# Attention over eight rows on one core: two finished key slots take row 7's layer 1 values, and every engine's order is written anew

## The chip, the core and the metric

The kernel runs on one of the eight cores of a Trainium2 chip. The core has TensorE (PE in the profile; PEld is its weight load), VectorE (DVE), ScalarE (ACT), GpSimd (POOL) and SyncE (SP), which here only issues DMAs. They run beside each other and wait for each other through semaphores. The metric is the device time of one execution in microseconds, as the median of several runs. Before the change it is 232.87 us (three runs: 232.79, 232.87 and 234.93).

## What is computed

Eight rows (a decode step: one token each) go twice through attention over a window of 1024 cached keys and values, and twice through a small dense block. Both attention layers use the same caches and weights.

```python
# x: [8, 1, 448]; k_cache, v_cache: [8, 8 heads, 4096, 256]; wq: [448, 4096]; wo: [4096, 448]
# w1: [448, 1792]; w2: [1792, 448]; everything is bf16
def A(x, k_cache, v_cache, wq, wo):
    q = (x @ wq) as [8, 16 heads, 1, 256]
    k, v = the last 1024 positions of the caches, each head used by two of q's
    p = softmax(q k^T / 16)
    return (p v) as [8, 1, 4096] @ wo
def B(x, w1, w2):
    return silu(x @ w1) @ w2
x = x + A(layernorm(x)); x = x + B(layernorm(x))      # layer 1
x = x + A(layernorm(x)); x = x + B(layernorm(x))      # layer 2
```

## The kernel before

Row by row, 8 key loads and 8 value loads of 512 KB go into a ring of 30 slots in SBUF (`slots`, line 456 issues the loads). SP issues them in a fixed order, and a load waits until the slot that it overwrites has been read for the last time. Row b's keys serve layer 1 and layer 2 of that row before they are freed; row 6's and row 7's slots are never overwritten, as no load follows them.

The program is a list of tasks. Each names the buffers that it reads and writes, from which `Plan` derives the waits, and `Plan.schedule` puts the tasks of each engine in an order that is written out by hand in `ORDER`: one character for each task, the place of the next task in the list of those that are left (in the order in which the program adds them). An engine works strictly in this order. A task whose input is late therefore holds everything behind it on its engine.

What a row does, with the names that the orders below use (a name with `:b` belongs to row b):

- `KT0` to `KT7` (line 632, DVE): two transposes for each key slot, in place, as soon as its load has landed.
- `S0.0`, `S0.1` (648, PE): the scores of layer 1 for the heads' first and second half; `S1.0`, `S1.1` those of layer 2. Each half is four groups of matmuls.
- `max`, `mT`, `mg`, `mb` (665 to 669, DVE), `exp` (672, ACT), `perm` (674, PE), `turn` (676, DVE), `l` (680, PE), `rl` (690, DVE): the softmax, with a 0 for layer 1 and a 1 for layer 2.
- `PVA` (729, PE): the values of heads 0 to 3. `PVD` (748): heads 4 to 7, one group of four matmuls a head. For rows 6 and 7 `PVC` takes heads 4 to 6, and `PVc` (760) head 7. `PV1.0` and `PV1.1` (729) are layer 2's values of the row before.
- `oevA`, `oevC`, `oevD`, `oev1` (715 and 723, ACT): copy the values from PSUM to SBUF; `oTA`, `oTC`, `oTD`, `oT1` (702, PE) turn them by a selection matmul; `oTev` (696, DVE) scales them. A and C work in two halves, `.0` and `.1`.
- `woA`, `woD`, `woC` (801, PE) and `woc` (816): the output projection; `rowb1` (1091, ACT), `fold1` (501, PE).
- `xb1` (827, DVE), `stat1` (834, PE), `var1` (837, ACT), `pow1` (839, POOL): norm; `w1` (518, PE), `yT` (538, DVE), `tanh` (846, ACT), `hT` (847, DVE), `w2` (865, PE), `rowb2` (869, ACT), `fold2`: the dense block. Then `xb2`, `stat2`, `wq0` and `wq1` (892, PE), `qT` (538, DVE), `qm` (901, DVE), `qd` (905, PE) and `qbd2` (909, ACT) make layer 2's queries, which `S1.0` waits for.
- `zero` (853, PE): matmuls whose result nobody reads.

At the start the norm and the queries of all eight rows are made together: `xb0` (576, DVE), `sq8` (547, ACT), `sqh8` (548 and 549, DVE), `stat8` (553), `x0` (580 to 587, DVE), `q1` (591, PE), `q1r`, `q1T`, `q1s` (595, 597, 610, DVE), `qbd1` (622, POOL). Constants are filled in by `init`, `initb` (a whole PSUM bank), `initq`, `inits` and `initz` on DVE. Sums over the rows of `wo` and `w2` are made once: `rsum` (443, ACT), `rsum2` and `rsum3` (435, DVE), and `rsumd` (438 and 447) writes them into the weights; `woD:0` and `w2:0` need them.

At the end, rows 0 to 6 go through their last projection and dense block together (`wo8`, `w18`, `z8`, `h8` at line 979, `w28` at 983, `xres8` at 988, `rowb9` at 991, `fold9` at 992, `orow8` at 994), and row 7 by itself (`woL`, `foldL`, `statL`, `w1L`, `w2L`, `orowL`).

The edited function is `o_turn`. With `halves`, its two copies go to `e_sb`. For layer 1 (`g` is None and `L` is 0) that is `E_sb[0]` for both halves, a part of `qbd[0]`, which had held the exponentials of layer 1: the second copy must wait until the first selection has read it.

Of the kernel before, what the change touches and what calls it, by code (L numbers as in the profile page):

```python
# [14 lines left out]

ORDER = {
    "pe": (
        "0000001000000000101111112222000200066000028827222010111117777000002444422100017777161551002010044000"
        "1005550000111117777000030444443200011661144410011101054000006055000011111777700003044443220001110033"
        "3302201100044000177005000011111777700040044444321001111444410201110100330010605500001111177770004004"  # L20
        "4444320001115144441001110110330010660500300111177770004004444322012228882041002222200004400000666600"
        "00cccc0000000500044443220001107066605504401200f0033bbb4390200500020144033555500111222244442211412321"
        "05044000100"),
    "dve": (
        "22Ca9BknxkDvv23iy1ArgCCCSk7Awodxr706t6Dtb1EDzBrraml2twi3l6hfhgl31o3kfaec2232ba99288442f514a403943822"
        "61203010098909706065ab09a90087700555504000100088909806065ab0a990087700555550000100088980878060aba0a9"
        "0087700555550000110a08989078060aba0ab0088700555550000100098980778005ab099b00777005555500001000989807"
        "78005aa0b9b00777005555500001000a90989078060aaba099a900005555500001100aaiba0cf0c8ba070600444030200002"
        "0111333311122211110000"),
    "act": (  # L30
        "0022223313333133d33b43222224211000000000201112100000000022011100000000002201100000000000220110000000"
        "00002201100000000000220111110000000002201100100000403020001110001010"),
    "pool": (
        "00000301022000110220022002200200001000"),
}


# [164 lines left out]
def bass_interleave_layers__sliding_block_cached__dense_activation_silu__decode_kernel(  # L202
# [3 lines left out]
    _, HKV, SK, DH = A_k_cache.shape  # L206
# [18 lines left out]
    LAST = NB - 1  # L225
# [10 lines left out]
    slots = [sb(f"slot{i}", [P, 2048], BF16) for i in range(R)]  # L236
# [44 lines left out]
    def QB(i, k2):  # L281
        return [("qbd", i, k2)]

    def bk(i):
        return [("bank", i)]

    def SL(s, h=None):
        return [("slot", s, 0), ("slot", s, 1)] if h is None else [("slot", s, h)]
# [4 lines left out]
    def dve(fn, reads, writes, row, name):  # L293
        add("dve", fn, reads=reads, writes=writes, row=row, name=name)

    def act(fn, reads, writes, row, name):
        add("act", fn, reads=reads, writes=writes, row=row, name=name)
# [152 lines left out]
    slot_of = {}  # L450
# [241 lines left out]
    def o_out(b, tb, n, o_c, dst, h0, keys, name, rk):  # L692
        if dst is None:
            act(lambda e: e.activation(o2[b], bank[tb][:, o_c:o_c + 2 * n], ACTF.Copy), bk(tb), keys, b, "oTc" + name)
            return
        dve(lambda e: e.tensor_tensor(  # L696
            dst, bank[tb][:, o_c:o_c + 2 * n].rearrange("p (a n) -> p a n", a=2),
            rl[b][:, h0:h0 + n].unsqueeze(1).broadcast_to([P, 2, n]), ALU.mult),
            bk(tb) + rk, keys, b, "oTev" + name)

    def o_sel(tb, src, s, sel_o, o_c, n, reads, b, name):
        pe([lambda e, a=a, s=s: e.matmul(bank[tb][:, o_c + a * n:o_c + (a + 1) * n], src(s)[:, a:DH:2], sel_o(s),  # L702
                                         start=(s == 0 and a == 0), stop=(s == 1), skip_group_check=True)
            for s in ((0, 1) if s is None else (s,)) for a in range(2)], reads + ["ident", "selb"], bk(tb), b, name)

    def o_turn(b, L, n, sel_o, o_c, dst, h0, keys, name, halves, g=None):

        pb, tb, qi, rk = (OB[L], LB[L], L, [("rl", b)]) if g is None else \
            ((OB[1], SC[1])[g], (LB[1], OB[1])[g], g, [("rlg", g)])
        ob = bank[pb]  # L710
        if halves:
            for s in range(2):
                e_sb, k = (E_sb[qi], QB(qi, 1)) if g is None or s == 0 else (pT_sb[qi], QB(qi, 0))
                if g is None or s == 0:
                    act(lambda e, s=s, e_sb=e_sb: e.activation(e_sb, ob[:, s * DH:(s + 1) * DH], ACTF.Copy), bk(pb), k, b,  # L715
                        "oev%s.%d" % (name, s))
                else:
                    dve(lambda e, s=s, e_sb=e_sb: e.tensor_copy(e_sb, ob[:, s * DH:(s + 1) * DH]), bk(pb), k, b,
                        "oev%s.%d" % (name, s))
                o_sel(tb, lambda s, e_sb=e_sb: e_sb, s, sel_o, o_c, n, k, b, "oT%s.%d" % (name, s))  # L720
        else:
            full = qbd[L][:, 8:8 + 2 * DH]
            act(lambda e: e.activation(full, ob[:, :], ACTF.Copy), bk(pb), QB(L, 0) + QB(L, 1), b, "oev" + name)  # L723
            o_sel(tb, lambda s: full[:, s * DH:(s + 1) * DH], None, sel_o, o_c, n, QB(L, 0) + QB(L, 1), b, "oT" + name)
        o_out(b, tb, n, o_c, dst, h0, keys, name, rk)
# [8 lines left out]
    def pv_first(b):  # L734
        lists = [pv(b, 0, j, j, 0, 8, 2 + 2 * j, 2, "") for j in range(4)]
        for i in range(4):
            pe([l[i] for l in lists], [k for kvh in range(4) for k in SL(slot_of[b, "v", kvh])] + QB(0, 0), bk(OB[0]), b,
               "PVA")
        o_turn(b, 0, 8, lambda s: view(ident[:], s, [(32, 4), (2, 2)]), C_O, oT1[b][:, :, 0:8], 0,
               [("oT1", b, kvh) for kvh in range(4)], "A", True)  # L740

    def pv_late(b, k0, k1, name):

        n = k1 - k0
        for i, kvh in enumerate(range(k0, k1)):
# [415 lines left out]
```

## Time and profile before

| | us |
|---|---|
| median of three runs | 232.87 |
| the profiled execution | 234.52 |
| its span on the core | 232.6 |
| TensorE busy | 168.7 |
| VectorE busy | 157.6 |
| ScalarE busy | 66.6 |
| POOL busy | 22.9 |
| transfers: mean rate over the span | 336 GB/s |

In the profile's text a line such as L632 is a line of the kernel, `slot<-slot` are the tiles written and read, and an arrow behind a row names what ended the idle time before it. The granted clock is the share of TensorE's full clock that it was given.

### The profile page before, as it was taken

Reading aid. Unit: us, or ns where it says so; the run is one execution under the profiler, and the core shown is the slowest. Engines: PE = TensorE matmul, PEld = TensorE weight load, DVE = VectorE, ACT = ScalarE, POOL = GpSimd, SP = SyncE. Lnnn points to the kernel's source line nnn. Section 1 sums busy time; section 2 is a strip of 40 time slices with the busy share of each in tenths; the row PEclk is TensorE's granted clock in tenths of the full one; section 3 lists DMA queues with packets and bytes.
Section 4 is the critical chain, followed back from the end, with each engine's and each line's share of the span. In section 5 each row is a group of like instructions: output and inputs, shape, how many; then the busy total and the mean of one; then the engine's idle time right before and its main releaser. Section 6 shows DMA issues by size and latency. Waiting matters only on the chain.

```text
span 232.6 us, 8240 instructions
## 1 busy us (share of the span) xinstructions
PE 168.7 (73%) x3648; PEld 95.8 (41%) x3648; DVE 157.6 (68%) x422; ACT 66.6 (29%) x203; POOL 22.9 (10%) x42
## 2 busy tenths in 40 slices
PE   1000526158897987988798889778888997999994
PEld 1000513112464444445444644444355465566553
DVE  5009899993983697498568747864996598354742
ACT  2000000997213322232332133223321431243321
POOL 1000201001100200020020002000200101001200
PEclk9999999656999999999999999999999999999999
DMA  6999999999999999999999999999999999600000
GB/s 155 387 409 410 380 380 399 405 409 410 403 392 386 413 405 352 391 411 408 359 402 409 405 359 407 410 370 379 409 409 387 409 380 407 229 0 6 3 1 4
DMA packets 23401, 78.20 MB, mean 336 GB/s; under 512 B 3127, under 2 KB 6086, under 8 KB 22982
## 3 DMA queue, kind: packets, MB, share of 16 engines
q1 hardware_dynamic: 22806, 77.30, 85.7%
q8 instruction: 28, 0.46, 0.8%
q10 hardware_dynamic: 560, 0.38, 0.8%
q14 instruction: 7, 0.06, 0.1%
HBM read 77.67 MB, written 0.01 MB: 334 GB/s over the span
## 4 chain that ended last, share of the span: by engine, by line
PE 45%; DMA 19%; ACT 13%; DVE 13%; SPq 5%; issue 4%; DVEq 0%
DMA w_sb<-in_B_w_dram 12%; PE bank L648 10%; DMA slot<-in_A_k_cache_dram 7%; PE bank L729 7%; DVE slot L632 6%; PE bank L892 6%; ACT slot L443 6%; PE bank L801 4%; SPq L456 3%; PE bank L518 3%; PE bank L865 2%; PE bank L748 2%; DVE bank L538 2%; PE bank L905 2%; ACT qbd L672 2%
## 5 line engine op out<-in xcount | busy, mean ns | idle before, releaser
L632 DVE STREAM_TRANSPOSE slot<-slot 128x512 uint32<-128x512 uint32 x128 | 81.6, 682 | 13.7 <-DMA slot<-in_A_k_cache_dram 13.2
L648 PE MATMUL bank<-slot,qbd 128*16 128x256 bf16 (+1 forms) x1024 | 39.4, 286 | 7.3 <-ACT qbd L909 3.3
L648 PEld LDWEIGHTS bank<-slot,qbd 128*16 128x16 bf16 (+1 forms) x1024 | 23.4, 88 | 17.4 <-ACT qbd L909 6.7
L729 PE MATMUL bank<-slot,qbd 128*4 128x512 bf16 (+1 forms) x384 | 26.9, 389 | 2.3 <-DVE qbd L676 1.6
L839 POOL TENSOR_TENSOR fcols<-fcols 128x1 f32<-128x1 f32 x17 | 9.5, 556 | 92.0 <-ACT fcols L837 81.9
L591 PE MATMUL bank<-slot,wq_sb 128*128 128x16 bf16 x128 | 3.6, 174 | 19.9 <-DVE slot L584 19.9
L622 POOL TENSOR_TENSOR qbd<-q1s,fcols 128x256 bf16<-128x256 bf16 x16 | 9.6, 614 | 85.7 <-PE bank L702 79.4
L892 PE MATMUL bank<-wq_sb,xbz 128*2 128x256 bf16 x512 | 16.1, 275 | 0.0
L909 ACT ACTIVATE qbd<-bank 128x256 bf16<-128x256 f32 x16 | 6.1, 384 | 34.2 <-PE bank L905 34.2
L696 DVE TENSOR_TENSOR q1s<-bank,q1s 128x16 bf16<-128x16 f32 (+1 forms) x18 | 3.0, 166 | 19.0 <-PE bank L702 19.0
L853 PE MATMUL bank<-ident,cols 128*128 128x512 bf16 x48 | 15.4, 387 | 0.0
L801 PE MATMUL bank<-wo_sb,q1s 128*1 128x449 bf16 x248 | 15.3, 377 | 0.2 <-ACT wo_sb L447 0.2
L715 ACT ACTIVATE qbd<-bank 128x256 bf16<-128x256 f32 x22 | 8.4, 383 | 18.9 <-PE bank L729 14.7
L443 ACT ACTIVATE slot<-w_sb 128x448 bf16<-128x448 bf16 x6 | 3.5, 576 | 35.6 <-DMA w_sb<-in_B_w_dram 35.4
L729 PEld LDWEIGHTS bank<-slot,qbd 128*4 128x4 bf16 (+1 forms) x384 | 8.2, 85 | 13.0 <-issue 3.1
L676 DVE STREAM_TRANSPOSE qbd<-bank 128x256 bf16<-128x256 bf16 x17 | 8.1, 476 | 8.0 <-PE bank L674 7.7
L538 DVE STREAM_TRANSPOSE bank<-bank 128x256 f32<-128x256 f32 (+1 forms) x25 | 10.8, 433 | 3.0 <-PE bank L892 1.1
L892 PEld LDWEIGHTS bank<-wq_sb,xbz 128*2 128x2 bf16 x512 | 11.7, 82 | 2.0
L591 PEld LDWEIGHTS bank<-slot,wq_sb 128*128 128x128 bf16 x128 | 3.5, 104 | 20.0 <-DVE slot L584 20.0
L723 ACT ACTIVATE qbd<-bank 128x512 bf16<-128x512 f32 x13 | 7.7, 595 | 11.7 <-PE bank L748 9.4
L665 DVE TENSOR_REDUCE mm<-bank 128x1 f32<-128x256 f32 x17 | 7.1, 418 | 5.5 <-PE bank L648 5.2
L748 PE MATMUL bank<-slot,qbd 128*12 128x512 bf16 (+3 forms) x120 | 9.9, 412 | 0.0
(163 smaller groups left out, 238.3 us busy)
## 6 DMA issues: line engine op xcount, KB each, us to landing
slot<-in_A_k_cache_dram SPq DMA_DIRECT2D x64, 512.0 KB, 8.4
slot<-in_A_v_cache_dram SPq DMA_DIRECT2D x64, 512.0 KB, 10.7
wo_sb<-in_A_wo_dram SPq DMA_DIRECT2D x1, 3584.0 KB, 26.0
wq_sb<-in_A_wq_dram SPq DMA_DIRECT2D x3, 1024.0 KB, 9.3
w_sb<-in_B_w_dram SPq DMA_DIRECT2D x1, 1568.0 KB, 28.3
w_sb<-in_B_w_dram SPq DMA_DIRECT2D x1, 1344.0 KB, 17.7
wq_sb<-in_A_wq_dram SPq DMA_DIRECT2D x1, 256.0 KB, 3.6
wq_sb<-in_A_wq_dram ACTq DMA_DIRECT2D x1, 256.0 KB, 4.0
```

Source lines behind the costliest of these rows:

```text
L443: act(lambda e, i=i, a=a: e.activation(junk, w[:, i * PW + R0 + a * D:i * PW + R0 + (a + 1) * D], ACTF.Copy, scale=-1.0 / D, accum_out=sum ...
L538: dve(lambda e: e.transpose(view(bank[bi][:], n, [(2, n // 32), (n // 16, 16), (1, 2)]), bank[bi][:, 0:n].rearrange("p (g r s) -> p g r s" ...
L622: pool(lambda e, k2=k2: e.tensor_tensor(qdata(0, k2), q1s[:, b, 64 * k2:64 * k2 + 64].rearrange("p (n r) -> p n r", r=2).unsqueeze(3) .bro ...
L632: dve(lambda e, v=v: e.transpose(v, v), SL(s, h), SL(s, h), b, "KT%d" % k)
L648: fns.append(lambda e, w=w, j=j, kv=kv, cb=cb, par=par: e.matmul(sc[32 * j:32 * j + up_to, 0:256], w, kv, start=(cb == 0 and par == 0), st ...
L715: act(lambda e, s=s, e_sb=e_sb: e.activation(e_sb, ob[:, s * DH:(s + 1) * DH], ACTF.Copy), bk(pb), k, b, "oev%s.%d" % (name, s))
L729: return [lambda e, u=u: e.matmul(bank[OB[L] if ob is None else ob][32 * j:32 * j + 2 * n, :], pT_sb[L if qi is None else qi][:, pcol(u, c ...
L748: pe([lambda e, t=t, c0=c0, w=w, kvh=kvh: e.matmul(bank[OB[0]][32 * t:32 * t + 2 * w, :], pT_sb[0][:, pcol(2 * t, c0):pcol(2 * t, c0) + 2 ...
L801: fns.append(lambda e, i=i, w=w, c0=c0: e.matmul(bank[XB][32 * (i % 4):32 * (i % 4) + 1, c0:c0 + D + 1], oT(i), w, start=(i < 4), stop=(i ...
L839: pool(lambda e: e.tensor_tensor(rhalf, var4, nhalf, ALU.pow), ["var4", "nhalf"], ["rhalf"], b, "pow" + name)
L853: pe(lambda e: e.matmul(bank[SC[1]][:, :], cols[:, 3:4].broadcast_to([P, P]), view(ident[:], 0, [(0, 4), (1, P)]), start=True, stop=True), ...
L892: pe([lambda e, j=j, c=c, s=s, wb=wb, k2=k2: e.matmul(bank[wb][32 * j:32 * j + 2, 0:256], pair(b, xcol(c, k2), s), view(wq_sb[:], c * HD + ...
```

## The change

Two things change. In `o_turn`, for row 7 in layer 1, the two halves of A go to the two halves of the slot that held row 6's key 6, and those of C to the slot of key 7. Layer 2 of row 7 and all other rows keep their buffers. And the four order strings are new: 238 of 511 places on PE hold another task than before, 232 of 422 on DVE, 25 of 168 on ACT and 12 of 38 on POOL. SP's order stays.

```diff
 ORDER = {
     "pe": (
-        "0000001000000000101111112222000200066000028827222010111117777000002444422100017777161551002010044000"
-        "1005550000111117777000030444443200011661144410011101054000006055000011111777700003044443220001110033"
-        "3302201100044000177005000011111777700040044444321001111444410201110100330010605500001111177770004004"
-        "4444320001115144441001110110330010660500300111177770004004444322012228882041002222200004400000666600"
-        "00cccc0000000500044443220001107066605504401200f0033bbb4390200500020144033555500111222244442211412321"
-        "05044000100"),
+        "000u000011110000002220110011151000100033399300611110111117777000030233332210011055040333302010003302"
+        "8010550000111117777000033033332200011666611002201120044000177716000001111777700704003333220001166151"
+        "4002201101044000177716000001111777700040044442320001161551400220110100022017771600000111177770004004"
+        "4442320001166114444100110000330017771611110111177770004004444232012228882041002222200000330017777102"
+        "00cccc00000005000444423200011880066660044012000033ccc43a02060500020144033555502h01122224444221131121"
+        "61551000000"),
     "dve": (
-        "22Ca9BknxkDvv23iy1ArgCCCSk7Awodxr706t6Dtb1EDzBrraml2twi3l6hfhgl31o3kfaec2232ba99288442f514a403943822"
...
+        "1iRJLBqN.17rcA10xExZpk0CT3rTqqiQgxxxh43flGgruunBtppC6rnvpnglsbkknbqpbbdl51h0dded68l76113c66668639a33"
...
     "act": (
-        "0022223313333133d33b43222224211000000000201112100000000022011100000000002201100000000000220110000000"
-        "00002201100000000000220111110000000002201100100000403020001110001010"),
+        "0022223313333423d33b42221111311000000000220110100000000022011000000000002201100000000000220110000000"
+        "00002201100000000000220111100000000002201000100000403020001111001000"),
     "pool": (
-        "00000301022000110220022002200200001000"),
+        "00000301022002200301022003010301001000"),
 }
...
         if halves:
             for s in range(2):
                 e_sb, k = (E_sb[qi], QB(qi, 1)) if g is None or s == 0 else (pT_sb[qi], QB(qi, 0))
+                if b == LAST and L == 0:
+                    sl = slot_of[LAST - 1, "k", 6 if name == "A" else 7]
+                    e_sb, k = slots[sl][:, 1024 * s:1024 * s + DH], SL(sl, s)
                 if g is None or s == 0:
```

What the strings say, read off for the stretches that matter below (`*4` is four in a row; `-` before, `+` after; fills left out where the line says so).

DVE from the first instruction to the first maximum, without `init`, `initb`, `initq`, `inits` and `initz`:

```text
- xb0 sqh8*2 KT1 st8*3 KT0 x0 KT3*2 KT0 KT2 x0*2 KT1 KT5 x0 st8 KT2 KT7 KT5 q1r q1T x0 KT4*2 q1s KT6*2 KT7 rsum3 max0
+ KT1*2 KT0 KT2 KT3 xb0 sqh8*2 KT2 st8 x0*2 KT3 x0 st8 KT6 x0 KT4 x0 st8 KT5 st8 x0 KT0 KT7*2 KT6 KT4 q1r q1T KT5 q1s rsum3 rsum2 max0
```

Before the first `KT1` stand 24 instructions in the old order and 8 in the new; between it and `max0` stand 62 and 78. After `max0` the old order mixes `rsum2` and `rsum3` with `mT0`, `mg0` and `mb0`; the new one has the three at once, then `turn0` and two `rsum3`. On ACT the first `exp0` stands behind six `rsum` of `w2` in both.

DVE in row 2 from the first norm to the queries, and PE in row 2:

```text
- xb1 KT2*2 KT3 yT KT3 hT KT4 KT5 KT4 xb2 KT6 KT5 qT0
+ xb1 KT2*2 yT KT3 hT KT3 KT4 KT5 xb2 KT6 KT5 KT6 qT0
- oTA.1 PVD*2 PV1.0*2 PVD*2 PV1.0*2 PV1.1 oTD woA woD PV1.1*3 fold1 zero oT1 w1 stat1 zero*4 w2 S0.0 fold2 S0.0*2 stat2 wq0 wq1 qd0 S0.0 S1.0*4
+ oTA.1 PVD*2 PV1.0*4 PVD*2 woA oTD PV1.1*2 woD PV1.1*2 zero fold1 oT1 stat1 w1 zero*3 w2 S0.0*3 fold2 S0.0 zero stat2 wq0 wq1 qd0 S1.0*4
```

PE in the other rows, from the late values to the projection:

```text
row 0 - PVD*4 xinit woA oTD zero woD fold1 zero stat1 w1 zero*4 w2
      + PVD*3 zero PVD woA oTD woD zero fold1 zero*2 stat1 w1 w2
row 1 - PVD PV1.0*4 PVD PV1.1 PVD PV1.1*2 PVD woA oTD PV1.1 woD
      + PVD*2 woA PV1.0*2 PVD PV1.0 PVD PV1.0 PV1.1*3 oTD PV1.1 woD
row 3 - PVD*3 woA PVD PV1.0*4 oTD PV1.1*2 woD PV1.1*2
      + PVD*2 PV1.0*2 PVD PV1.0 PVD PV1.0 woA oTD PV1.1*2 woD PV1.1*2
row 4 - PVD*4 PV1.0*4 oTD woA PV1.1 woD PV1.1*3
      + PVD*2 PV1.0 PVD PV1.0*2 PVD PV1.0 woA oTD PV1.1*2 woD PV1.1*2
row 5 - PVD*3 PV1.0 PVD PV1.0*3 PV1.1 oTD woA woD PV1.1*3
      + PVD*2 PV1.0*2 PVD*2 PV1.0*2 PV1.1*2 oTD woA woD PV1.1*2
row 6 - fold2 stat2 wq0 wq1 S0.1:7*4
      + fold2 zero wq1 stat2 wq0 S0.1:7*4
```

Row 7: ACT's copies, PE around them, and the end on PE:

```text
- oevA.0 exp1:6 oevA.1 oevC.0 lc1:6 oevC.1      + oevA.0 exp1:6 oevA.1 lc1:6 oevC.0 oevC.1
- oTA.1 PVC*2 woA PV1.0 PVC PV1.0*3 oTC.0 PV1.1*2 oTC.1 PV1.1*2 woC PVc
+ oTA.1 PVC*2 PV1.0*2 woA PVC PV1.0*2 PV1.1*2 oTC.0 oTC.1 PV1.1*2 woC PVc
- w28 xres8 perm1a l1a ... woLa xinitL fold9 zero foldL zero*2 statL w1L xres zero w2L zero
+ w28 perm1a xinitL xres8 l1a ... woLa zero foldL zero*2 statL fold9 w1L xres w2L zero*2
```

`h8` on DVE stands before `mT1a` in the old order and behind `mg1a` in the new one.

More of the change, by code (lines that the diff above doesn't have):

```diff
@@ L23 @@
-        "05044000100"),
-    "dve": (
-        "22Ca9BknxkDvv23iy1ArgCCCSk7Awodxr706t6Dtb1EDzBrraml2twi3l6hfhgl31o3kfaec2232ba99288442f514a403943822"
[L26 to L29, printed above, removed]
+        "000u000011110000002220110011151000100033399300611110111117777000030233332210011055040333302010003302"
@@ new lines @@
+        "8010550000111117777000033033332200011666611002201120044000177716000001111777700704003333220001166151"
[3 more added lines that the diff above has]
+        "61551000000"),
+    "dve": (
+        "1iRJLBqN.17rcA10xExZpk0CT3rTqqiQgxxxh43flGgruunBtppC6rnvpnglsbkknbqpbbdl51h0dded68l76113c66668639a33"
+        "63563440c0aa2199170055aa0c9a0078700555550000110089908708065ba0a990077700555550002000088880770605ab0c"
+        "aa0077700555550000000908889077005ab09a9007770055555000000090a980877005ab09aa007870055555000000090888"
+        "9078005aa09b900987005555500000000990988078060bcaa0ab990000555550000100bdc0aafc09c09a0806004440302000"
+        "022201333312122211110000"),
```

## The prediction

> **What bounds the kernel now.** I read the page first, then the chain of waits, the waits of the engines, and last the timeline in the stretches that the chain names.
>
> ```profile
> span 232.6 us, 8240 instructions
> PEclk9999999656999999999999999999999999999999
> GB/s 155 387 409 410 380 380 399 405 409 410 403 392 386 413 405 352 391 411 408 359 402 409 405 359 407 410 370 379 409 409 387 409 380 407 229 0 6 3 1 4
> PE 45%; DMA 19%; ACT 13%; DVE 13%; SPq 5%; issue 4%; DVEq 0%
> slot<-in_A_k_cache_dram SPq DMA_DIRECT2D x64, 512.0 KB, 8.4
> DVE slot L632 <- DMA slot<-in_A_k_cache_dram: 13.2, 2, 12.1
> ```
>
> The stream of keys and values runs at some 410 GB/s until it ends in the 35th slice. At that rate a load of 512 KB takes 1.28 us and the 16 loads of a row 20.5 us. Yet the chain is 45% TensorE and only 19% transfers, and VectorE waited for a key slot only twice, 12.1 of 13.2 us being the first key of all. So a row is paced by its own chain of work, with the transfers just ahead of it. The chain in order of time shows this, and below it stands one stretch of the table of windows (TensorE, weight loads, VectorE, ScalarE and POOL busy, granted clock, transfers):
>
> ```profile
> 55.60 1.45 PE bank L801 x14
> 87.73 0.39 ACT qbd L909
> 99.34 1.30 DVE slot L632 x2
> 109.11 0.39 ACT qbd L909
> 130.25 0.39 ACT qbd L909
> 143.83 1.99 DVE slot L632 x3
> 152.07 0.39 ACT qbd L909
> 173.83 0.39 ACT qbd L909
> ```
>
> ```profile
> 40.27:55.46 15.19, 7.40 (x62) 2.26 (x62) 11.74 (x20) 14.78 (x51) 0.34 (x1) 0.59 1.02 407
> ```
>
> The first release of layer 2's queries (L909) marks each row. The distances are 21.4, 21.1, 21.8 and 21.8 us: 0.9, 0.6, 1.3 and 1.3 over the 20.5 of the stream. Before them ScalarE, which sums weight rows (L443), is busy 14.78 of the 15.19 us up to 55.46, and then releases row 0's projection (L801, 55.60).
>
> **The change part by part.** The profiled execution took 234.52 us, of which its span is 232.6; the three runs have a median of 232.87 (232.79 to 234.93). I sum differences against the span and put them on the median.
>
> *The buffer.* Row 7's four copies (two in A, two in C) go to slots of row 6's keys 6 and 7, so the second copy of a pair need not wait for the selection matmul that reads the first. No instruction is added.
>
> ```profile
> 200.63 0.38 ACT L715 ACTIVATE qbd<-bank 128x256 bf16<-128x256 f32 x1 [2.38 <-PE bank L729]
> 200.91 0.47 ACT L672 ACTIVATE qbd<-bank,mm 128x256 bf16<-128x256 f32 x1
> 201.36 0.38 ACT L715 ACTIVATE qbd<-bank 128x256 bf16<-128x256 f32 x1
> 204.56 0.38 ACT L715 ACTIVATE qbd<-bank 128x256 bf16<-128x256 f32 x1 [0.31 <-PE bank L702]
> 205.56 0.74 PE L801 MATMUL bank<-wo_sb,q1s 128*1 128x449 bf16 x12
> ```
>
> In pair A the exponential of row 6 (200.91, 0.47) stands between the copies in ScalarE's order, before and after. It ends at 201.38 and the second copy starts then anyway: nothing is gained, and if the exponential were gone the copy would wait for the first selection. In pair C the second copy waited 0.31 us for TensorE. That wait goes; the copy of row 6's sums (L687) also moves ahead of the pair. TensorE then has both selections after two value groups and one gap less: I take 0.2 us of the 0.31 off L801 at 205.56. Writing a slot is costed at zero: the copy has the same shape, and every reader of those keys stands before it in TensorE's order. A slower write would be bounded by one copy, 0.38.
>
> *The last 15 us.* Two moves cost there. The last fold of rows 0 to 6 (L992) moves from before row 7's fold to between the variance and the up projection; the activation h8 (L979) moves behind two softmax steps, so the down projection of rows 0 to 6 (L983) starts later.
>
> ```profile
> 218.88 0.94 PE L983 MATMUL bank<-w_sb,slot 128*7 128x448 bf16 x14
> 225.72 0.35 PE L992 MATMUL bank<-slot 128*7 128x448 bf16 x1
> ```
>
> L983 (218.88) moves back about 0.3, an estimate from the steps that h8 now waits for, but the permutation behind it waits for ScalarE's exponential anyway, and the residual matmuls now follow that permutation instead of preceding it: +0.05. The fold takes 0.35 of TensorE's time, partly hidden where it stands, since row 7's fold waits there for ScalarE; where it goes nothing hides it but the overlap of two matmuls: +0.1. Together with the pair, the tail comes to -0.05, between -0.3 (all of 0.31) and +0.6 (both moves in full, no gain).
>
> *The start.* Before the first key's transpose VectorE now has 8 instructions instead of 24. The norm of all rows (xb, L576, and its two squares) is put behind five transposes.
>
> ```profile
> 4.38 0.20 DVE L576 TENSOR_TENSOR xb<-bank,fcols 128x40 bf16<-128x40 f32 x1
> 5.09 0.19 DVE L549 TENSOR_TENSOR slot<-slot 128x32 bf16<-128x32 f32 x1
> 17.36 0.71 DVE L632 STREAM_TRANSPOSE slot<-slot 128x512 uint32<-128x512 uint32 x1 [12.08 <-DMA slot<-in_A_k_cache_dram]
> 18.13 0.06 DVE L331 MEMSET fcols<- 32x4 f32 x1
> 18.93 0.48 DVE L331 MEMSET bank<- 128x512 f32 x1
> 39.40 0.42 DVE L665 TENSOR_REDUCE mm<-bank 128x1 f32<-128x256 f32 x1
> 40.27 2.02 DVE L435 TENSOR_REDUCE slot<-w_sb 128x4 f32<-128x1792 bf16 x1
> 44.35 0.46 ACT L672 ACTIVATE qbd<-bank,mm 128x256 bf16<-128x256 f32 x1
> 196.04 0.41 DVE L665 TENSOR_REDUCE mm<-bank 128x1 f32<-128x256 f32 x1
> 196.94 0.21 DVE L669 STREAM_TRANSPOSE mm<-mg 128x32 f32<-128x32 f32 x1
> ```
>
> ```profile
> 17.36:39.40 22.04, 8.21 (x224) 6.48 (x224) 20.80 (x63) 0.00 (x0) 2.85 (x3) 1.00 1.04 391
> ```
>
> From 17.36 to the first maximum (39.40) VectorE ran 63 instructions, busy 20.80 of 22.04 us. In the new order 79 stand there: a weight sum that is now ahead of the maximum (2.0), the norm with its round trip to ScalarE (4.38 to 5.28: 0.9), two bank fills (0.5 each), a dozen small fills (0.06 to 0.1 each, say 0.8), less three moved behind (0.6). That is 4.1 us: the maximum comes at 43.5. The three steps after it take 1.1 us with it in row 7 (196.04 to 197.15), so the exponential can start at 44.65. ScalarE reaches it at 44.35. So a delay that looks like 4 us costs 0.3, since ScalarE had its sums to do; and all behind it on ScalarE, up to the release at 55.60, moves by the same 0.3. With the weight sums that VectorE still owes I take 0.4. The ends are 0 (the fills overlap better; a gain is excluded, since ScalarE had no idle time there to give back) and 2.5 (in the rivals). The same order puts one small weight step before row 0's first turn: +0.15. Start: +0.55.
>
> *Row 2.* Here the old order put the variance matmuls (L834) behind the up projection, and VectorE's third key behind a late transfer.
>
> ```profile
> 101.06 0.95 PE L518 MATMUL bank<-w_sb,xbz 128*2 128x224 bf16 x32
> 101.93 0.25 PE L834 MATMUL bank<-xbz 128*128 128x1 bf16 x4
> 102.53 0.39 DVE L538 STREAM_TRANSPOSE bank<-bank 128x224 f32<-128x224 f32 x1
> 103.21 0.27 ACT L846 ACTIVATE th<-bank,fcols 128x14 f32<-128x14 f32 x1 [0.72 <-POOL fcols L839]
> 103.59 0.17 DVE L847 SCALAR_TENSOR_TENSOR q1s<-th,bank 128x14 bf16<-128x14 f32 x1
> ```
>
> L518 ended at 102.0 but was turned at 102.53, and the tanh waited 0.72 us for POOL's power of that late variance. The new order has the variance first and two transposes, not three, before the turn. The turn can start at 102.2, the tanh at 102.65, and L847 follows one transpose (0.71 as at 17.36) at 103.2: -0.4. One transpose more stands before the query turn, so the gain could shrink to 0.1; I keep -0.4.
>
> *Rows 1 and 3 to 6.* Groups of value matmuls change places with the output projection.
>
> ```profile
> 118.40 1.03 PE L729 MATMUL bank<-slot,qbd 128*8 128x512 bf16 x16
> 117.42 0.93 PE L801 MATMUL bank<-wo_sb,q1s 128*1 128x449 bf16 x16
> ```
>
> Four groups take 1.03, so one takes at most 0.26 us; the projection takes 0.93 less its overlap, say 0.8. Row 1's last late-value group had seven groups of row 0 ahead of it; now three and a projection: -0.1. Row 3 is nearly level (-0.1). Row 4 had its four late groups together; now three others come among them (up to +0.6), but the same work stood behind them before the projection could start, so +0.15. Row 5 has one more ahead: +0.1. Row 6 keeps its groups; its second query half goes first while the variance waits, and VectorE's transposes end both at 194.8. I call these rows 0, between -0.6 and +0.6. No load changes its place in SP's queue: value slots come free a few groups earlier or later, under 1 us, against the 8.4 us from issue to landing that the page shows where a load alone would need 1.28, so several loads stand ahead of each.
>
> *Sum.* +0.55 - 0.4 + 0 - 0.05 = +0.1, against a span of 232.6; on the median I say 232.9 us: no change that can be told.
>
> **The rivals.**
>
> *Slower: the norm behind the keys.* The point of decision is ScalarE's 44.35. The durations of the old 63, added up row by row from 17.36 to 39.40, make 24.2 us, and they took 22.0. If the new 79 don't overlap, they take 24.2 + 4.1 = 28.3: the maximum is at 45.7, the exponential at 46.85. ScalarE stands 2.5 us, and all of row 0 moves. With +0.15 and -0.4 - 0.05 that is 232.87 + 2.2 = 235.1. Against it: the old ones did overlap.
>
> *Slower: TensorE stays cold.* In the slices from 40.7 to 58.2 the granted clock was 0.6, 0.5 and 0.6, and full after. By the row of 40.27 to 55.46 it was 0.59 while TensorE was busy 7.40 of 15.19. The new order takes one filler matmul from between row 0's last selection and its projection, and four from behind L518. If the clock rises later, L518 (0.95 in row 2) takes twice as long, with the folds around it some +1.3 us: 234.2. The Trainium skill (TensorE: Matmul & The Clock Gate, Part 1, What's actually happening) says that the clock doubles after a busy window of about 3.4 us and falls after an idle one, in windows that run freely. By that rule a hole ahead of row 0 can cost one whole window; the trace agrees so far as the clock was down from the slice at 40.7 us, and up again only when TensorE's work had closed up by 58 us.
>
> *Faster: the rows fall to the stream's pace.* If the new orders take out what the four distances have over 20.5 us (0.9 + 0.6 + 1.3 + 1.3 = 4.1), the time is 228.9. For it: 99.34 and 143.83 are transposes behind late transfers, which a shorter row would release sooner. Against it: only row 2 has a wait that the order visibly removes.
>
> *The edit does nothing.* Pair C's wait of 0.31 becomes idle time in front of L801, as pair A's already is, and the orders cancel: 232.9 to 233.2.
>
> **How the numbers follow.** Forecast 0.60 (232.9, its own range 231.9 to 234.0, from the ends of rows and tail); no effect 0.08; norm late 0.13; cold clock 0.07; stream's pace 0.12. About 1% (2.3 us) is what a measurement of this kernel can tell from no change: faster takes the stream's pace, 0.12; slower half of the norm's, which lies at the bound of 235.2, and as much for it or the other losses together with the cold clock, 0.12; the same 0.76. The range leaves out most of the fastest case and the slow end: 231.2 to 234.8.
>
> **What would show it.** In the changed profile the first exponential on ScalarE starts at 44.4 to 45.2, with an idle time before it under 1 us, and the output projection of row 0 at 55.8 to 56.4. In row 2 the tanh no longer waits for POOL. L715's fourth copy in row 7 follows the third at once, the second still follows the exponential. The row marks lie 21 to 21.8 apart. I am wrong if ScalarE idles over 2 us ahead of that exponential, if the granted clock is half beyond 58 us, or if the marks come 20.5 apart.

## The result and the profile after

| | before | after |
|---|---|---|
| median of 20 runs | 234.39 us (231.87 to 236.12) | 235.14 us (234.03 to 237.65) |
| ratio, with its 95% interval | | 1.0065 (1.0040 to 1.0089) |
| profiled execution, its span | 234.52, 232.6 | 234.37, 232.6 |

The change makes the kernel slower by 1.5 us by the ratio (0.0065 of 234.39; 0.9 to 2.1), and by 0.75 between the two medians. The ratio is taken over the executions that were not slow as a whole, and is not the quotient of these medians. The loss is small, less than the 1% that the prediction called a change that can be told, but its interval leaves out 0, and the forecast had no change. Note also that the kernel before, run 20 times, stands at 234.39 and not at the 232.87 of the three runs on which the forecast was put. The forecast of 232.9 misses 235.14 by 2.2 us, and about two thirds of that is this base.

The profiled executions are no help at their ends: both spans are 232.6, because the one of after is among its shortest. They have to be read stretch by stretch. From the page of the changed kernel:

```profile
span 232.6 us, 8240 instructions
PEclk9999999956999999999999999999999999999999
GB/s 162 391 407 411 380 381 397 408 407 409 411 362 306 411 408 392 364 414 409 391 387 413 409 348 407 409 404 405 407 410 387 405 394 404 225 3 3 3 4 1
PE 55%; DVE 20%; ACT 11%; issue 5%; DMA 5%; SPq 1%; DVEq 0%
```

Two things differ from before. The chain's share of transfers fell from 19% to 5% and VectorE's rose from 13% to 20%. And the transfers, which ran at 392 and 386 GB/s in the 12th and 13th slice, now dip to 362 and 306 there: slots of the first row come free later (SP issues the keys that follow at 70.43 us, and at 68.67 before). The chain of waits in order of time says where VectorE came in. First the start of the chain before, then of the chain after (start, length, what):

```profile
11.95 28.30 DMA w_sb<-in_B_w_dram
40.27 0.68 ACT slot L443 x2
```

```profile
4.29 12.62 DMA slot<-in_A_k_cache_dram
16.94 0.71 DVE slot L632
...
37.55 0.69 DVE q1s L610
...
42.86 1.88 DVE slot L435
...
46.95 0.68 ACT slot L443 x2
...
57.06 0.96 PE bank L804 x15
```

Before, the first 40 us hang on one thing: the load of w2, whose rows ScalarE then sums, until row 0's projection (the 55.60 of the prediction). After, the chain goes from the first key through VectorE's whole list to the first exponential, and only then joins ScalarE's sums. The timeline of the changed kernel has the join, and the windows view has VectorE's work ahead of it (TensorE, weight loads, VectorE, ScalarE and POOL busy, clock, transfers):

```profile
39.51 0.58 ACT L443 ACTIVATE slot<-w_sb 128x448 bf16<-128x448 bf16 x1 [16.16 <-DMA w_sb<-in_B_w_dram]
42.77 1.96 DVE L435 TENSOR_REDUCE slot<-w_sb 128x4 f32<-128x1792 bf16 x1
44.65 0.41 DVE L665 TENSOR_REDUCE mm<-bank 128x1 f32<-128x256 f32 x1
45.79 0.47 ACT L672 ACTIVATE qbd<-bank,mm 128x256 bf16<-128x256 f32 x1 [2.11 <-DVE mm L669]
```

```profile
16.94:44.65 27.71, 9.51 (x242) 7.27 (x242) 25.07 (x79) 4.25 (x13) 2.85 (x3) 1.00 1.04 395
```

ScalarE is done with six sums at 43.68 and stands 2.11 us for the softmax's last step on VectorE. The exponential comes at 45.79 instead of 44.35, row 0's projection at 57.06 instead of 55.60. From the one to the other it is 11.27 us, and 11.25 before: what stands behind the exponential moves with it.

The two profiles close as follows. Layer 2's queries of row 0 are released at 67.17 instead of 66.23 (+0.94; the projection itself took less time after). From there to row 6's release it is 129.13 instead of 130.24 (-1.11), row 7's part takes 19.18 instead of 19.40 (-0.22), and from there to the last output it is 14.92 instead of 14.54 (+0.38). The rows of the first and last releases, before and after:

```profile
66.23 0.38 ACT L909 ACTIVATE qbd<-bank 128x256 bf16<-128x256 f32 x1 [2.24 <-PE bank L905]
...
196.47 0.38 ACT L909 ACTIVATE qbd<-bank 128x256 bf16<-128x256 f32 x1 [3.13 <-PE bank L905]
...
215.87 0.39 ACT L909 ACTIVATE qbd<-bank 128x256 bf16<-128x256 f32 x1 [1.76 <-PE bank L905]
```

```profile
67.17 0.38 ACT L912 ACTIVATE qbd<-bank 128x256 bf16<-128x256 f32 x1 [2.07 <-PE bank L908]
...
196.30 0.38 ACT L912 ACTIVATE qbd<-bank 128x256 bf16<-128x256 f32 x1 [2.69 <-PE bank L908]
...
215.48 0.38 ACT L912 ACTIVATE qbd<-bank 128x256 bf16<-128x256 f32 x1 [1.69 <-PE bank L908]
```

The middle is not what it seems, though: most of the 1.11 is two rows of the old kernel that stalled in this one execution (below).

### The profile page after: what moved, and what is told of

Same layout as the page of the kernel before. It is cut to its first block, busy times and chain, and to the rows that moved or that the text cites. A ratio compares the mean times of both kernels' runs of the same rounds, so it can differ in the third digit from the quotient of the medians.

```text
span 232.6 us, 8240 instructions
## 1 busy us (share of the span) xinstructions
PE 169.5 (73%) x3648; PEld 95.0 (41%) x3648; DVE 158.1 (68%) x422; ACT 66.1 (28%) x203; POOL 22.9 (10%) x42
## 4 chain that ended last, share of the span: by engine, by line
PE 55%; DVE 20%; ACT 11%; issue 5%; DMA 5%; SPq 1%; DVEq 0%
PE bank L648 11%; DVE slot L632 9%; PE bank L732 9%; PE bank L895 6%; PE bank L804 5%; DMA slot<-in_A_k_cache_dram 5%; PE bank L751 4%; ACT qbd L672 3%; PE bank L856 3%; PE bank L518 3%; ACT slot L443 2%; PE bank L674 2%; ACT rowb L1094 2%; PE bank L702 2%; PE bank L908 2%
## 5 line engine op out<-in xcount | busy, mean ns | idle before, releaser
L732 PE MATMUL bank<-slot,qbd 128*4 128x512 bf16 (+1 forms) x384 | 27.6, 388 | 1.0 <-DVE qbd L676 0.8
L895 PE MATMUL bank<-wq_sb,xbz 128*2 128x256 bf16 x512 | 16.6, 275 | 0.2 <-DVE xbz L830 0.2
L856 PE MATMUL bank<-ident,cols 128*128 128x512 bf16 x48 | 16.3, 392 | 0.0
L912 ACT ACTIVATE qbd<-bank 128x256 bf16<-128x256 f32 x16 | 6.1, 383 | 33.8 <-PE bank L908 33.8
L538 DVE STREAM_TRANSPOSE bank<-bank 128x256 f32<-128x256 f32 (+1 forms) x25 | 11.0, 440 | 2.6 <-PE bank L518 2.1
L718 ACT ACTIVATE qbd<-bank 128x256 bf16<-128x256 f32 x18 | 6.9, 381 | 15.9 <-PE bank L732 14.5
L751 PE MATMUL bank<-slot,qbd 128*12 128x512 bf16 (+3 forms) x120 | 10.5, 411 | 0.0
L868 PE MATMUL bank<-w_sb,q1s 128*1 128x449 bf16 x98 | 6.5, 353 | 4.9 <-DVE q1s L850 4.9
L672 ACT ACTIVATE qbd<-bank,mm 128x256 bf16<-128x256 f32 x17 | 8.0, 470 | 6.7 <-DVE mm L669 6.1
```

Source lines behind the costliest of these rows:

```text
L538: dve(lambda e: e.transpose(view(bank[bi][:], n, [(2, n // 32), (n // 16, 16), (1, 2)]), bank[bi][:, 0:n].rearrange("p (g r s) -> p g r s" ...
L672: act(lambda e: e.activation(E, x, ACTF.Exp, bias=m[:, 0:1], scale=1.0, **acc), bk(si) + [("mm", si)], QB(qi, 1) + ([] if acc == {} else [ ...
L732: return [lambda e, u=u: e.matmul(bank[OB[L] if ob is None else ob][32 * j:32 * j + 2 * n, :], pT_sb[L if qi is None else qi][:, pcol(u, c ...
L751: pe([lambda e, t=t, c0=c0, w=w, kvh=kvh: e.matmul(bank[OB[0]][32 * t:32 * t + 2 * w, :], pT_sb[0][:, pcol(2 * t, c0):pcol(2 * t, c0) + 2 ...
L856: pe(lambda e: e.matmul(bank[SC[1]][:, :], cols[:, 3:4].broadcast_to([P, P]), view(ident[:], 0, [(0, 4), (1, P)]), start=True, stop=True), ...
L895: pe([lambda e, j=j, c=c, s=s, wb=wb, k2=k2: e.matmul(bank[wb][32 * j:32 * j + 2, 0:256], pair(b, xcol(c, k2), s), view(wq_sb[:], c * HD + ...
```

## The experiments

**Which part of the change.** The new orders split cleanly where the same tasks are done in both: the start (up to row 0's second fold), the end (from row 7's first projection), and the rows between.

```diff
 new start:  - old, old, old      + start new, rows old, end old
 new end:    - old, old, old      + start old, rows old, end new
 new rows:   - old, old, old      + start old, rows new, end old  (old buffers)
 old start:  - new, new, new      + start old, rows new, end new  (new buffers)
```

> The kernel before with the new order of the start alone (VectorE up to row 1's first keys, TensorE up to row 0's second fold, ScalarE up to row 0's last weight sum). Theory 1 (the loss is the start: VectorE reaches the first maximum late and ScalarE stands about 2 us ahead of the first exponential): +0.9 to +1.6 us on the kernel before, and row 0's projection at about 57 us. Theory 2 (the loss is the new orders of rows 1 to 6): +-0.3. Theory 3 (the loss is the end, where the activation of rows 0 to 6 and the last fold have moved): +-0.3, and the late start is eaten by the transfers that run ahead.

> The kernel before with the new order of the end alone (TensorE from row 7's first projection, VectorE and ScalarE from row 7's dense block). Theory 1: 0 to +0.4 us. Theory 2: +-0.2. Theory 3: +1.0 to +1.6.

> The kernel before with the new orders between these two alone (rows 1 to 6 and row 7's layer 1; the old buffers). Theory 1: -0.8 to 0 us, as row 2's and row 4's waits go. Theory 2: +0.9 to +1.6. Theory 3: +-0.4.

> The changed kernel (new buffers too) with the old order of the start. Theory 1: -0.6 to +0.2 us against the kernel before, so 1 us or more under the changed kernel. Theories 2 and 3: +1.0 to +1.6, as the changed kernel.

Against the kernel before (233.86 us in these runs): new start 1.0087 (1.0048 to 1.0125), which is +2.0 us; new end 1.0014 (0.9973 to 1.0055); new rows 1.0003 (0.9963 to 1.0042); the changed kernel with the old start 0.9974 (0.9935 to 1.0013), which is -0.6. Put alone, the start brings the whole loss, and taken out of the change, the loss is gone. Theories 2 and 3 fall. The size was missed: +2.0 lies above the +0.9 to +1.6 of theory 1, and the +0.1 of the new rows just above its -0.8 to 0. The new start alone has the idle time of the changed kernel, and a little more:

```profile
39.59 0.58 ACT L443 ACTIVATE slot<-w_sb 128x448 bf16<-128x448 bf16 x1 [15.78 <-DMA w_sb<-in_B_w_dram]
...
46.26 0.47 ACT L672 ACTIVATE qbd<-bank,mm 128x256 bf16<-128x256 f32 x1 [2.50 <-DVE mm L669]
```

**What in the start.** Four kernels change VectorE's list only, against the kernel before or the new start.

```diff
 new VectorE start (TensorE and ScalarE old)
-  VectorE: old list
+  VectorE: new list
 sum ahead (from the kernel before)
-  rsum3 max0 mT0 rsum2 mg0 mb0 rsum3 rl0 turn0
+  rsum3 rsum3 max0 mT0 rsum2 mg0 mb0 rl0 turn0
 sum behind (from the new start)
-  rsum3 ... rsum2 max0 mT0 mg0 mb0 rsumd turn0 rsum3
+  rsum3 ... max0 mT0 mg0 mb0 rsum2 turn0 rsumd rsum3
 norm first (from the new start)
-  8 fills, KT1, 8 fills, KT1 KT0 KT2 KT3 ... xb0 sqh8*2 ...
+  7 fills, 9 fills that the norm needs, xb0 sqh8*2, KT1, ...
```

> The kernel before with the new start, but VectorE's one weight sum of w2 that the new order has ahead of the first maximum stands behind the softmax's last step (as does its write into the weights). The norm and the queries stay as late as in the new start. Theory 1a (what costs is only how much work VectorE has in its order ahead of the first exponential): first maximum at about 42.7 us, ScalarE idle under 0.4 us ahead of the exponential, 0 to +0.5 us on the kernel before. Theory 1b (the late norm and queries cost by themselves, through TensorE's late scores): +1.2 to +2.0, as the new start. Theory 1c (the new start's orders of TensorE and ScalarE cost): +1.2 to +2.0.

> The kernel before, in which one weight sum of VectorE (2.9 us) is moved from behind the first softmax to ahead of its maximum; norm, queries, fills and all other engines stay. Theory 1a: the last softmax step ends at about 45.5 instead of 42.6, ScalarE reaches the exponential at 44.35 and stands some 1.1 us, and the time is +0.9 to +1.5 us. Theories 1b and 1c: +-0.3.

> The kernel before with the new start, but the norm (three instructions) and the nine fills that it needs stand ahead of the first key's transpose, in time that VectorE idles anyway. This takes about 2.7 us of work out of the stretch ahead of the maximum; the weight sum stays ahead of it. Theory 1a: maximum at about 42, ScalarE idle under 0.4 us, 0 to +0.4 us on the kernel before. Theory 1b: the same. Theory 1c: +1.2 to +2.0.

> The kernel before with VectorE's new start alone (one small fill of the denominators' columns stands a little earlier, as TensorE's old order needs it); TensorE and ScalarE keep the old order. Theories 1a and 1b: +1.2 to +2.0 us. Theory 1c: -0.3 to +0.4.

| kernel | ratio (95% interval) | us | ScalarE idle ahead of the exponential | exponential after ScalarE's first sum |
|---|---|---|---|---|
| before | 1 | 0 | 0 | 4.08 |
| new start | 1.0087 (1.0048 to 1.0125) | +2.0 | 2.50 | 6.67 |
| new VectorE start | 1.0085 (1.0047 to 1.0123) | +2.0 | 2.36 | 6.54 |
| changed kernel | 1.0065 (1.0040 to 1.0089) | +1.5 | 2.11 | 6.28 |
| sum ahead | 1.0033 (0.9994 to 1.0073) | +0.8 | 1.52 | 5.69 |
| sum behind | 1.0045 (1.0012 to 1.0079) | +1.1 | 0.93 | 5.11 |
| norm first | 1.0013 (0.9992 to 1.0033) | +0.3 | 0 | 4.15 |

The last column is the fair one, as w2 lands at another time in each execution (39.2 to 40.6 over the profiles). The new VectorE list alone costs as much as the whole new start, so the orders of TensorE and ScalarE are out (theory 1c). The time goes up with how late the exponential is, whichever instruction is put ahead of it. The rate is only roughly known, 0.5 to 1.0 us per us: 2.0 for 2.59 in the new start, 0.8 for 1.61 in sum ahead, 1.1 for 1.03 in sum behind. In sum ahead nothing but one weight sum has moved; the norm and the queries are where they were. Its +0.8 is a little under the +0.9 to +1.5 of theory 1a and has an interval that just reaches 0, so by itself it would not settle it:

```profile
39.17 0.58 ACT L443 ACTIVATE slot<-w_sb 128x448 bf16<-128x448 bf16 x1 [34.34 <-DMA w_sb<-in_B_w_dram]
...
44.86 0.47 ACT L672 ACTIVATE qbd<-bank,mm 128x256 bf16<-128x256 f32 x1 [1.52 <-DVE mm L669]
```

Sum behind gave back about half. Theory 1a expected nearly all (0 to +0.5 us, ScalarE idle under 0.4) and theory 1b nothing, so neither is right alone. Its timeline says why:

```profile
38.20 0.69 DVE L610 CAST q1s<-bank 128x512 bf16<-128x512 f32 x1 [0.17 <-PE bank L602]
...
44.02 0.42 DVE L665 TENSOR_REDUCE mm<-bank 128x1 f32<-128x256 f32 x1 [0.50 <-PE bank L648]
...
45.18 0.47 ACT L672 ACTIVATE qbd<-bank,mm 128x256 bf16<-128x256 f32 x1 [0.93 <-DVE mm L669]
```

With the sum out of the way the maximum waits for TensorE's scores, because the queries (L610) are cast at 38.20, where the kernel before has them at 33.93. So theory 1b has a part: the late norm is the next limit. By itself it still makes the exponential 1.03 late (5.11 less 4.08 in the table). With the norm first and the sum left in its place, ScalarE doesn't wait, but only just: the maximum comes at 42.86 and not at the 42 that was expected, and VectorE's last step ends at 43.96, 0.03 us ahead of the exponential.

**The buffers by themselves, and the repairs.**

```diff
 buffers alone:         the edit of o_turn, all orders old
 changed, norm first:   the changed kernel, VectorE's start as in norm first
 changed, both repairs: the same, and rsum2 behind mb0 as in sum behind
```

> The kernel before with the buffers alone: row 7's layer 1 copies go to the slots of row 6's keys 6 and 7; all orders are the old ones. If the buffers do what the prediction says: pair C's second copy follows the first at once but for the copy of row 6's sums between them, the projection L801 of row 7's pair C stands 0.2 to 0.4 us earlier against pair A's first selection, pair A is unchanged, and the time is -0.4 to +0.2 us. If they do nothing, the idle time in front of the second copy turns into idle time of TensorE: 0 at that projection.

> The changed kernel, but the norm and the fills that it needs stand ahead of the first key's transpose. Theory 1a: ScalarE does not idle ahead of the first exponential, and the time is -0.7 to +0.3 us on the kernel before (as the changed kernel with the whole old start), 1 to 2 us under the changed kernel. If the loss has a second part that does not show there (the order of the keys, fills that now stand late): +0.8 or more on the kernel before.

> As the changed kernel with the norm first, and VectorE's weight sum of w2 also behind the softmax. The softmax's last step then ends about 2 us earlier than ScalarE comes to the exponential. Theory 1a: this gives nothing more, within 0.4 us of the kernel with the norm first, as ScalarE's own sums set the time. If VectorE's path to the exponential counts by itself: another 1 to 2 us less.

Buffers alone measured 1.0020 (0.9987 to 1.0053), +0.5 us with an interval that holds 0. ScalarE no longer waits for TensorE between pair C's copies, and yet the pair gains nothing: from pair A's first selection (L702) to the projection (the L801 of before) it takes 4.48 us, and 4.49 before. First the selection of the kernel before (its projection is the 205.56 of the prediction); then, from the timeline of buffers alone, TensorE's pair A selection, ScalarE's second copy, TensorE's projection:

```profile
201.07 0.21 PE L702 MATMUL bank<-ident,qbd 128*128 128x8 bf16 x2
```

```profile
201.56 0.21 PE L702 MATMUL bank<-ident,slot 128*128 128x8 bf16 x2
...
204.62 0.39 ACT L718 ACTIVATE slot<-bank 128x256 bf16<-128x256 f32 x1
...
206.04 0.74 PE L804 MATMUL bank<-wo_sb,q1s 128*1 128x449 bf16 x12
```

With the old order TensorE has two value groups between the selections, and they cover the wait. With the new order the selections are neighbours and nothing covers it. New rows without the buffers (first), and the changed kernel (second), from pair A's first selection again:

```profile
199.44 0.21 PE L702 MATMUL bank<-ident,qbd 128*128 128x8 bf16 x2 [0.17 <-ACT qbd L715]
203.81 0.20 PE L702 MATMUL bank<-selb,qbd 128*128 128x6 bf16 x2 [0.47 <-ACT qbd L715]
204.38 0.74 PE L801 MATMUL bank<-wo_sb,q1s 128*1 128x449 bf16 x12
```

```profile
200.91 0.21 PE L702 MATMUL bank<-ident,slot 128*128 128x8 bf16 x2 [0.17 <-ACT slot L718]
204.60 0.26 PE L702 MATMUL bank<-selb,slot 128*128 128x6 bf16 x4
205.22 0.74 PE L804 MATMUL bank<-wo_sb,q1s 128*1 128x449 bf16 x12
```

That is 4.94 and 4.31 us, against 4.49 before. The order alone loses 0.45, the buffers alone win nothing, and both together win 0.18: they are one change. The other profiles agree. From row 6's release of the queries to row 7's it is 19.39 to 19.45 us in the seven with the old rows and buffers, 19.39 with the buffers alone, 19.82 with the new rows alone, and 19.12 to 19.18 in the five with both. (The description of the kernel before says that no slot of row 6 is overwritten. The ring has 30 slots, so row 7's last two value loads do overwrite those of row 6's keys 0 and 1; for keys 6 and 7, which the change uses, it holds.)

The changed kernel with the norm first measured 1.0007 (0.9974 to 1.0040), with both repairs 0.9995 (0.9963 to 1.0028). Neither interval holds the 1.0065 of the change, though that of the first touches the change's own (1.0040 to 1.0089). With the norm first alone ScalarE still waits 0.27 us for VectorE, where no wait was expected. As theory 1a expects, the second repair adds nothing that can be told: with both, VectorE's last step ends at 41.83, 1.6 us before ScalarE gets there, and ScalarE's sums set the exponential. First the exponential with the norm first, then VectorE's last step and the exponential with both repairs:

```profile
43.69 0.47 ACT L672 ACTIVATE qbd<-bank,mm 128x256 bf16<-128x256 f32 x1 [0.27 <-DVE mm L669]
```

```profile
41.62 0.21 DVE L669 STREAM_TRANSPOSE mm<-mg 128x32 f32<-128x32 f32 x1
...
43.41 0.46 ACT L672 ACTIVATE qbd<-bank,mm 128x256 bf16<-128x256 f32 x1
```

**Everything that holds, together.**

```diff
 best: the changed kernel
-  start new, end new
+  start with both repairs, end old
```

> The changed kernel with both repairs of the start (norm first, the weight sum of w2 behind the softmax) and the old order of the end (TensorE from row 7's first projection, VectorE and ScalarE from its dense block); rows 1 to 6, row 7's layer 1 and its buffers stay as changed. If the parts add up: 0 from the start, -0.3 us from rows 1 to 6, -0.2 from pair C, 0 from the end (row 7 to the last output within 0.1 us of the kernel before, not 0.4 above it): -0.5 us on the kernel before, between -1.2 and +0.4. If the end's new order is worth something that its traces don't show: 0 or above.

It measured 0.9974 (0.9942 to 1.0006): 0.6 us under the kernel before, where 0.5 was expected. Its interval lies under the changed kernel's, as that of the changed kernel with the old start does. From the kernel before neither is told apart.

## Why the prediction was wrong, by its own steps

**The start is the step that failed.** It said +0.55; alone it measures +2.0 (1.1 to 2.9), and ScalarE's idle time, which it put at 0.3, is 2.11 in the changed kernel. The mechanism was right (VectorE reaches the first exponential later than ScalarE does), and its size was not. The work was summed rightly, and two other errors make the difference:

- *The work was right.* 4.1 us more were forecast for VectorE ahead of the maximum, and its busy time went from 20.80 to 25.07: 4.27. So was the delay behind the exponential, which reaches the projection unchanged; the 0.25 that the term added for weight sums and a weight step does not show there.
- *The idle time between instructions was left out.* The old list stands idle 1.24 of its 22.04 us (the row in the prediction), the new one 2.64 of 27.71 (the windows row above). Among the 1.40 us more are 0.29 in which the late norm waits for ScalarE's square and 0.17 ahead of the queries' cast; of the other 0.94, 0.65 stands in front of the additional fills. A small fill that has such a gap costs 0.055 to 0.08 us of idle time beside its 0.06 of work. With the 0.17 more of work, and the key 0.42 sooner (16.94 for 17.36), this makes the maximum 1.15 later than the 43.5 that was forecast.
- *ScalarE's arrival was taken as fixed.* The 44.35 is the landing of w2 plus six sums. In the changed kernel's profile w2 is there at 39.51, not 40.27, and ScalarE is at the exponential at 43.68. That is another 0.67. Added up: 0.3 + 1.15 + 0.67 = 2.12.

The margin on which "a delay that looks like 4 us costs 0.3" stood was the difference of two arrival times from one execution, where each moves by half a microsecond and more from one run to the next. The prediction had the other outcome among its rivals, as the norm behind the keys, with 2.5 us of idle time and +2.2 on the kernel before, and put 0.13 on it. That rival was the right one in its place and nearly in its price, and wrong in its reason, so that the price was partly luck: its exponential, at 46.85, was 1.06 too late, and ScalarE's arrival, at 44.35, 0.67 too late as well. It let all of the old overlap go. The overlap stayed. The durations of the new list, added up row by row, make 28.2 against 25.07 busy, 3.2 us of overlap, where the old one had 3.4 (24.2 and 20.80). What grew is the idle time beside it.

**The base failed too, and it is the larger part of the miss.** The forecast stands on a median of three runs, 232.87, and twenty gave 234.39. From that base the same sum says 234.5, with a range of 232.7 to 236.3 in which 235.14 lies. That the time fell out of the range is due to the base; that the change costs something, to the start.

**The buffers: right.** Pair A gained nothing, and pair C 0.18 of the 0.2 that was forecast. The prediction counted on the new order of the selections for it; the two halves above show that it takes both.

**Row 2: right in its place, and given back.** From the norm to the second norm it was to gain 0.4. Before, then after (VectorE's norm, its second norm, ScalarE's release of the queries):

```profile
100.56 0.20 DVE L827 SCALAR_TENSOR_TENSOR xbz<-bank,fcols 128x5 bf16<-128x5 f32 x1
...
105.85 0.23 DVE L827 SCALAR_TENSOR_TENSOR xbz<-bank,fcols 128x5 bf16<-128x5 f32 x1
```

```profile
101.62 0.20 DVE L830 SCALAR_TENSOR_TENSOR xbz<-bank,fcols 128x5 bf16<-128x5 f32 x1
...
106.49 0.23 DVE L830 SCALAR_TENSOR_TENSOR xbz<-bank,fcols 128x5 bf16<-128x5 f32 x1 [0.28 <-PE bank L503]
...
109.92 0.38 ACT L912 ACTIVATE qbd<-bank 128x256 bf16<-128x256 f32 x1 [2.25 <-PE bank L908]
```

5.29 became 4.87, which is -0.42. But the stretch ahead of it, from row 1's release (87.73; 88.57 after), grew from 12.83 to 13.05 (value groups and the projection have changed places there; which of them costs it was not tried), and the stretch behind it, from the second norm to the release at 109.11 and 109.92, grew from 3.26 to 3.43: three transposes stand ahead of the query turn. The prediction named this last cost and set it aside. The whole row went from 21.38 to 21.35. Over all profiles the part from the norm to the second norm takes 5.29 to 5.31 in the eight with the old rows and 4.59 to 4.87 in the six with the new ones, so this gain is there each time; the whole row takes 21.33 to 21.49 in the old ones and 21.14 to 22.21 in the new ones.

**Rows 1 and 3 to 6: nothing, as forecast.** In the profiled pair they gain 1.1, but the old kernel's rows 4 and 5 take 21.82 and 21.76 there, and 21.14 and 21.32 at their best in the eight profiles with the old rows. Single rows stall by 0.3 to 2.3 us in one execution and not in the next (row 4 of the changed kernel with both repairs took 23.38). With the shortest of each row over the profiles added up, from row 0's release to row 6's, the old rows take 128.84 and the new ones 128.49. The timed difference of new rows, 1.0003, agrees.

**The end: too cheap.** It said +0.15 for the two moves; in this pair of profiles it is +0.38. From layer 1's last product (L974) over the first selection of the permutation, row 7's norm and its turn to the last output, before, then after:

```profile
217.47 0.26 DVE L974 TENSOR_TENSOR slot<-bank,slot 128x98 f32<-128x98 f32 x1
219.93 0.28 PE L674 MATMUL bank<-qbd,perm 128*128 128x256 bf16 x1
226.59 0.23 DVE L827 SCALAR_TENSOR_TENSOR xbz<-bank,fcols 128x5 bf16<-128x5 f32 x1 [0.85 <-PE bank L503]
228.06 0.43 DVE L538 STREAM_TRANSPOSE bank<-bank 128x224 f32<-128x224 f32 x1 [0.72 <-PE bank L1032]
230.41 0.62 SPq L1049 DMA_DIRECT2D out_dram<-slot  x1
```

```profile
217.08 0.26 DVE L977 TENSOR_TENSOR slot<-bank,slot 128x98 f32<-128x98 f32 x1
219.68 0.28 PE L674 MATMUL bank<-qbd,perm 128*128 128x256 bf16 x1
226.35 0.23 DVE L830 SCALAR_TENSOR_TENSOR xbz<-bank,fcols 128x5 bf16<-128x5 f32 x1 [0.85 <-PE bank L503]
228.05 0.43 DVE L538 STREAM_TRANSPOSE bank<-bank 128x224 f32<-128x224 f32 x1 [0.23 <-PE bank L1035]
230.40 0.62 SPq L1052 DMA_DIRECT2D out_dram<-slot  x1
```

12.94 became 13.32. The permutation (L674) comes 2.60 behind that product instead of 2.46: 0.14 for the 0.05 forecast for the move of h8. From the norm to the turn (L538) it is 1.70 instead of 1.47: 0.23 for the 0.1 forecast for the fold, which now stands there at the head of the up projection. The two moves were not tried apart. The best kernel, with the old end, is back at 12.98 (216.03 to 229.01). The timed runs of new end can't tell this (+0.3 us, with an interval from -0.6 to +1.3), but the profiles can: 12.92 to 12.98 in the nine with the old end, and 13.32 to 13.49 in the five with the new one.

**The forecast signs.** The exponential was to start by 45.2 and came at 45.79, with the idle time over 2 us that was named as the sign of being wrong; the projection came at 57.06, not by 56.4. The tanh of row 2 is no longer released by POOL, pair C's copies follow each other at once, and the marks lie 21.1 to 21.4 apart in rows 1 to 5, as said. TensorE did not stay cold: its half clock fills two slices of the page instead of three (more on this below). And the edit does do something, only not by itself.

## What to carry to other kernels

A delay that another engine's work seems to cover is worth its margin, and a margin between two arrival times is known no better than those arrivals repeat: look at it in several executions before it is called 0.3. When instructions are added to a busy stretch, count the gap in front of each small one beside its duration. And where an order and a buffer change together, price them as one: each alone can be worth nothing, or less.

## What the runs showed of the hardware

The granted clock's dip around 45 to 58 us comes in some executions of a kernel and not in others. The changed kernel's 20 runs have mean clocks of 0.975 to 0.978 in nine and 0.993 to 1.0 in eleven, and the new start alone ran its profiled execution at full clock (1.000). How far the mean falls goes with the start, though: of the 102 runs with VectorE's new start, repaired or not, none is below 0.970; of the 172 with the old one whose clock is on record 57 are, down to 0.949. So the new start makes the dip shorter, where a rival of the prediction had a longer one; why it does was not tried. In the changed kernel the medians of the two groups are 235.75 and 234.89 us, but in the new start alone the ten runs with the dip have 235.49 and the two without it 236.52, so what the dip costs stays open. Profiled executions have means of 0.971, 0.978 and 0.992, which over some 232 us are 13.5, 10.2 and 3.7 us at half clock. The Trainium skill (TensorE: Matmul & The Clock Gate, Part 1, What's actually happening) has the clock decided in free-running windows of 3.4 us, and these are four, three and one of them; the trace agrees.

Small fills on VectorE came in two kinds: in the changed kernel's 28 ahead of the first maximum, 16 began before the instruction ahead of them had ended, and 12 stood 0.055 to 0.08 us behind it. The seven fills of a whole bank there all stood 0.1 us behind. The Trainium skill (VectorE: DVE Perf Modes, Two Vector instructions with no wait between them) says that an instruction whose operands start in another group of partitions than the last ones in that memory is held until all before it are done. No run here sorted the fills by that rule, so whether it explains the 1.40 us more of idle time stays open.
